# A sparse attention and feed-forward kernel: splitting its weights two tiles at a time

## The chip, the cores and the metric

The kernel runs on one core of one Trainium2 chip. The metric is the device time of one execution in microseconds (us), and lower is better. Shown with a kernel is the median of several executions; the profile is that of one further execution.

## The reference

Block-sparse attention over 4 batches, 8 heads, 768 positions and head size 64 is followed by a feed-forward layer over all 3072 tokens. Only the feed-forward part matters for the change:

```python
def _moe_ref(x, w_in, w_out):
    h = x @ w_in                                              # 3072x512 @ 512x2048
    sp = np.maximum(h, 0.0) + np.log1p(np.exp(-np.abs(h)))
    g = h * erf(sp)
    return (g @ w_out).astype(np.float32)                     # 3072x2048 @ 2048x512
```

The weights `w_in` and `w_out` are random float64 arrays. The attention output, with a batch's heads side by side, is `x`.

## The kernel before

**Precision.** TensorE multiplies f16 operands. So that little is lost, every f32 weight is scaled by a power of two and split into two f16 numbers: a high half, which is the rounded scaled weight, and a low half, which is what the rounding left. Three products (high by high, high by low, low by high) then stand for one.

**The weights.** Each weight is 16 tiles of 128 x 512. `weights()` (L512) is a generator that handles them in 17 steps, two neighbouring tiles (a pair) per step: steps 0 to 7 read `w_in`, steps 8 to 15 read `w_out`. A step decodes the float64 words to f32 on VectorE (`decode`, L418) and sums their squares on ScalarE (`square`, L437). From the sums come powers of two as scales: two for `w_in` (`scale_half`, L484, for 8 tiles each) and eight for `w_out`, one for each pair (`scale_pair`, L475, through a small TensorE matmul with ones, then `scale_part`, L469). `scale_part` runs three operations on a 128 x 1 column: exponent, scale and inverse scale. `ratios` (L488), after the last step, turns the inverse scales into the factors that `ff_gate` (L756) needs, and into `unscale` for the output.

**The split.** `halves` (L443) gives three views of tile i: the f32 tile, its high half and its low half. `high` (L451) is one ScalarE activation per tile, which copies with the scale from a 128 x 1 column and writes f16. For `w_out` the low half is one VectorE operation per tile (`low`, L455): weight times scale minus high half. For `w_in` the low half is made on TensorE: `rest` (L500) multiplies the f32 tile by a diagonal matrix of scales into PSUM, `rest_low` (L504) subtracts the high half by a matmul with minus the unit matrix, and `rest_out` (L507) copies the result out on ScalarE. The PSUM tag that `rest` and `scale_pair` use has two buffers.

**Places.** The halves are written over the buffer that holds the f32 weights. Slot n of a weight's buffer is 512 f32 wide. For `w_in` the f32 tile i lies in slot i + 1 and its halves go to slot i; for `w_out` the f32 tile lies in slot i + 2 (`APART`, L374). So the high half of `w_in` tile i + 1 overwrites a part of f32 tile i, and may be written only once `rest(i)` has read that.

**Order.** `weights()` is advanced three steps after each of the first six attention units (L917 to L940) and then run to its end (L944). Up to there, and through the first three rounds of the loop behind, a planner that simulates the engines chooses the order of TensorE, ScalarE and VectorE instructions; parts under `tc.high_priority()` go ahead. GpSimd and SyncE keep the order of the program. From round 3 of the main loop on (`held`, L960) all engines keep it.

**Main loop (L958).** Each round does `ff_first` (L710) for one group (24 matmuls into one of three PSUM tiles `h`), `ff_logs` (L734, five ScalarE activations, the first of which reads `h`), attention products of an older unit (`values`, L640), scores of a new one (`scores`, L608), `ff_second` (L765, 24 matmuls) for the group three rounds back, and `ff_gate` for the group two rounds back, whose first operation `y<-y,h` is the last reader of `h`. `gathers` (L807) brings the next blocks of V by DMAs that GpSimd and SyncE issue; a buffer for them is free when `values` has read it.

Of the kernel before, what the change touches and what calls it, by code (L numbers as in the profile page):

```python
# [10 lines left out]
I32 = mybir.dt.int32  # L11
BF16 = mybir.dt.bfloat16
AF = mybir.ActivationFunctionType
ALU = mybir.AluOpType
# [17 lines left out]
def sparse_attention_moe(ctx: ExitStack, tc: tile.TileContext, qT, kT, v, sampled, w_in, w_out, out):  # L32
# [7 lines left out]
    class InOrder:  # L40
# [15 lines left out]
    pe, act, dve, pool, sp = (  # L56
        InOrder(e, queued if e in (nc.sync, nc.gpsimd) else held) for e in (nc.tensor, nc.scalar, nc.vector, nc.gpsimd, nc.sync)
    )
# [54 lines left out]
    for n in range(P // BLOCK):  # L113
        part = slice(n * BLOCK, (n + 1) * BLOCK)
# [80 lines left out]
    def pow2_bound(bound, tag, by_sum):  # L195

        top = st.tile([P, 1], F32, tag="top", name=f"top_{tag}")
        dve.reduce_max(top, bound, AX.X)  # L200
        if by_sum:
            allm = ps_h.tile([P, W], F32, tag="h", name=f"allm_{tag}")
            if tag[0] == "v":
                pe.matmul(allm[0:1, 1 : 1 + P], top, eye, start=True, stop=True)
                top = st.tile([P, 1], F32, tag="top", name=f"most_{tag}")[0:1]
                dve.reduce_max(top, allm[0:1, 1 : 1 + P], AX.X)
            allm = allm[:, :1]
            pe.matmul(allm, ones[: top.shape[0]], top, start=True, stop=True)
        else:
            allm = st.tile([P, 1], F32, tag="allm", name=f"allm_{tag}")  # L210
            pool.partition_all_reduce(allm, top, P, bass.bass_isa.ReduceOp.max)
        return allm
# [161 lines left out]
    APART = {"i": 1, "o": 2}  # L374

    def weight_tile(name, n):
        return cp.tile([P, n + APART[name[1]], 512], F32, tag=name, name=name)

    NG = DFF // 512
    wi = weight_tile("wi", NK * NG)  # L380
    wo = weight_tile("wo", NF)
    wi16 = wi.rearrange("p n c -> p (n c)").bitcast(F16).rearrange("p (n c) -> p n c", c=1024)
    wo16 = wo.rearrange("p n c -> p (n c)").bitcast(F16).rearrange("p (n c) -> p n c", c=1024)
# [34 lines left out]
    def decode(key, i):  # L418

        first = i + APART[key]  # L420
        t = wi if key == "i" else wo
        w32 = t[:, first : first + 2, :].rearrange("p n c -> p (n c)")
        parts = [raw for n in (i, i + 1) for raw in places.pop((key, n), [])]
        mag = mags[(i // 2) % 2]
        c = 0
        for raw in parts:
            w = raw.shape[1] // 2
            raw = raw.rearrange("p (n w) -> p n w", w=2)
            lo, hi = raw[:, :, 0], raw[:, :, 1]
            m = mag[:, c : c + w]  # L430
            dve.tensor_scalar(m, hi, 3, 0x3FFFFFFF, ALU.logical_shift_left, ALU.bitwise_and)
            dve.scalar_tensor_tensor(m, hi, -0x40000000, m, ALU.bitwise_and, ALU.bitwise_or)
            done = w32[:, c : c + w].bitcast(I32)
            dve.scalar_tensor_tensor(done, lo, 29, m, ALU.logical_shift_right, ALU.bitwise_or)
            c += w

    def square(key, i):  # L437
        first = i + APART[key]
        w32 = (wi if key == "i" else wo)[:, first : first + 2, :].rearrange("p n c -> p (n c)")
        sq = mo.tile([P, 512], F32, tag="s", name=f"sq_{key}{i}", bufs=3).bitcast(BF16)  # L440
        act.activation(sq, w32, AF.Square, accum_out=wsq[key][:, i // 2 : i // 2 + 1])

    def halves(key, i):  # L443
        t, t16 = (wi, wi16) if key == "i" else (wo, wo16)
        return t[:, i + APART[key], :], t16[:, i, :512], t16[:, i, 512:]

    def scale_of(key, i):
        n = i // (2 * NK) if key == "i" else i // 2
        return (si if key == "i" else so)[:, n : n + 1]

    def high(key, i):  # L451
        w32, hi16, _ = halves(key, i)
        act.activation(hi16, w32, AF.Copy, scale=scale_of(key, i))

    def low(key, i):  # L455
        w32, hi16, lo16 = halves(key, i)
        dve.scalar_tensor_tensor(lo16, w32, scale_of(key, i), hi16, ALU.mult, ALU.subtract)

    NP = NF // 2
    eo, so, io = (sums[:, 16 + n * (NP + 2) : 16 + (n + 1) * (NP + 2)] for n in range(3))  # L460
    si, ii = so[:, NP:], io[:, NP:]
    sos, so = so, so[:, :NP]
# [4 lines left out]
    unit23 = float(1 << 23)  # L467

    def scale_part(total, n):  # L469
        e, sc, inv = eo[:, n : n + 1].bitcast(I32), sos[:, n : n + 1].bitcast(I32), io[:, n : n + 1].bitcast(I32)  # L470
        dve.tensor_scalar(e, total.bitcast(I32), 24, None, ALU.logical_shift_right)
        dve.tensor_scalar(sc, e, -unit23, (127 + 13 + 63) * unit23, ALU.mult, ALU.add)
        dve.tensor_scalar(inv, e, unit23, (127 - 13 - 63) * unit23, ALU.mult, ALU.add)

    def scale_pair(i):  # L475
        n = i // 2
        total = ps_o.tile([P, DM], F32, tag="o", name=f"total_{i}")[:, :1]
        pe.matmul(total, ones, wsq["o"][:, n : n + 1], start=True, stop=True)
        scale_part(total, n)

    def bound_part(part):
        return pow2_bound(wsq["i"][:, part * NK : (part + 1) * NK], f"wi{part}", True)

    def scale_half(total, part):  # L484
        scale_part(total, NP + part)
        dve.tensor_scalar(diag, eye, si[:, part : part + 1], None, ALU.mult)

    def ratios():  # L488
        dve.tensor_reduce(least[:, 0:1], si, AX.X, ALU.min)
        dve.tensor_scalar(rest_i, ii, least[:, 0:1], 2.0**-H_SHIFT, ALU.mult, ALU.mult)  # L490
        dve.tensor_reduce(least[:, 1:2], so, AX.X, ALU.min)
        for part in range(2):
            c = slice(part * NP // 2, (part + 1) * NP // 2)
            dve.tensor_scalar(ratio[:, c], io[:, c], least[:, 1:2], rest_i[:, part : part + 1], ALU.mult, ALU.mult)
        dve.tensor_scalar(least.bitcast(I32), least.bitcast(I32), -1.0, 254 * unit23, ALU.mult, ALU.add)
        dve.tensor_tensor(unscale, least[:, 0:1], least[:, 1:2], ALU.mult)
# [3 lines left out]
    def rest(i):  # L500
        rests[i] = ps_o.tile([P, DM], F32, tag="o", name=f"rest_{i}")
        pe.matmul(rests[i], diag, halves("i", i)[0], start=True, stop=False)

    def rest_low(i):  # L504
        pe.matmul(rests[i], less16, halves("i", i)[1], start=False, stop=True)

    def rest_out(i):  # L507
        act.activation(halves("i", i)[2], rests.pop(i), AF.Copy)
# [3 lines left out]
    def weights():  # L512
        loads = {5: (("o", 0),), 6: (("o", 2),), 7: (("o", 4), ("o", 6)), 10: (("o", 8),), 11: (("o", 10),)}
        sum_i = None
        for n in range(17):
            key, i = "io"[n // 8 % 2], n % 8 * 2
            if n in (4, 9):
                with tc.high_priority():
                    scale_half(sum_i, n // 8)
            pair = None  # L520
            if 5 <= n < 9:
                pair = 2 * (n - 5)
            if 10 <= n < 14:
                pair = 2 * (n - 6)
            if pair is not None:
                for part in range(2):
                    rest(pair + part)
                    high("i", pair + part)
            if n < 16:
                decode(key, i)  # L530
            if pair is not None:
                for part in range(2):
                    rest_low(pair + part)
                    rest_out(pair + part)
            if n < 16:
                square(key, i)
            if n >= 9:
                i = 2 * (n - 9)
                scale_pair(i)
                high("o", i)  # L540
                high("o", i + 1)
                low("o", i)
                low("o", i + 1)
            for piece in loads.get(n, ()):
                load_w(*piece)
            if n in (3, 7):
                sum_i = bound_part(n // 4)
            yield
        ratios()

    softs = {}
# [330 lines left out]
    def later(n=1):  # L882
        for _ in range(n):
            next(wgen, None)

    wgen = weights()
    for pr in range(HP):
        load_k(0, pr)
# [69 lines left out]
    for m in range(len(groups) + FF_LAG):  # L958
        ch, i = divmod(m, NGR)
        held[0] = m >= FF_LAG  # L960
        steps = 0
        if ch < len(until):
            first = until[ch - 1] if ch else FIRST
# [5 lines left out]
        last = groups[m - GATE_LAG] if GATE_LAG <= m < len(groups) + GATE_LAG else None  # L969
# [76 lines left out]
```

## Time and profile before

| | |
|---|---|
| median of 3 runs | 812.88 us (805.91 to 815.5) |
| the profiled execution | 810.12 us |
| its span, first to last instruction | 808.3 us |
| TensorE busy | 726.3 us (90%) |
| ScalarE busy | 601.6 us (74%) |
| VectorE busy | 560.3 us (69%) |
| GpSimd busy | 198.3 us (25%) |
| mean granted TensorE clock | 0.949 |

PE is TensorE's matmuls, PEld its weight loads, ACT is ScalarE, DVE is VectorE, POOL is GpSimd, SP is SyncE. The profile names an operation by its output and inputs in the program's tile names (`wi<-wi,sums` is `high` of `w_in`, `wo<-wo,sums` on ACT is `high` and on DVE `low` of `w_out`, `rest<-wi,room` is `rest` and `rest_low`). Nearly all rows carry L48, the line of a helper that issues everything, so one goes by tile names. The profiled execution was 2.76 us below the median of the three runs.

### The profile page before, as it was taken

The numbers are of one execution on the slowest core, as the hardware profiler recorded it, in microseconds if no ns is written. First come the engines' busy times: TensorE is split into PE (matmuls) and PEld (weight loads), VectorE is DVE, ScalarE is ACT, GpSimd is POOL, SyncE is SP. The second block draws the span as 40 slices with busy tenths as digits, with TensorE's granted clock in tenths as the row PEclk, the third lists the DMA queues.
The fourth block names the chain that finished last, engine by engine and source line by source line (L and its number), as shares of the span: only waits on it lengthen the run. The fifth ranks groups of instructions, "written<-read, shape, count | busy, mean of one in ns | idle before, by whom it ended". The sixth has DMA issues, their size and how long they took to land.

```text
span 808.3 us, 26228 instructions
## 1 busy us (share of the span) xinstructions
PE 726.3 (90%) x11136; PEld 510.3 (63%) x11136; DVE 560.3 (69%) x1043; ACT 601.6 (74%) x1035; POOL 198.3 (25%) x397
## 2 busy tenths in 40 slices
PE   1457787789978999999989999999999999999997
PEld 1435555556745776666767767667777776666663
DVE  7795898657756776766668768666767776564543
ACT  3656799567856788777867977877878878777674
POOL 3248410212333432400133423210333310000000
PEclk9558998979999999999999999999999999999999
DMA  9999654997499997953498997844598647312100
GB/s 315 398 258 294 202 116 76 145 241 166 119 218 182 171 274 185 203 132 81 92 206 182 215 212 185 190 97 98 130 191 180 149 113 181 73 28 48 9 27 26
DMA packets 188053, 129.45 MB, mean 160 GB/s; under 512 B 137760, under 2 KB 160928, under 8 KB 186912
## 3 DMA queue, kind: packets, MB, share of 16 engines
q1 hardware_dynamic: 173440, 83.98, 49.4%
q10 hardware_dynamic: 8608, 25.96, 10.7%
q0 software_dynamic: 5888, 17.84, 9.1%
q8 instruction: 87, 1.43, 0.7%
q14 instruction: 30, 0.25, 0.1%
HBM read 82.81 MB, written 12.95 MB: 118 GB/s over the span
## 4 chain that ended last, share of the span: by engine, by line
PE 74%; DMA 8%; issue 8%; DVE 5%; POOL 3%; ACT 1%; SPq 1%; POOLq 0%; ACTq 0%; DVEq 0%
PE h L48 29%; PE o L48 29%; PE s_m L48 8%; PE po_None L48 4%; PE s_f L48 3%; DMA qt<-in_qT_dram 2%; DMA xT<-x 2%; POOL kg L48 2%; DMA vbuf<-vtab,idx 1%; DVE room L48 1%; PE po L48 1%; DMA pT_f<-p_f 1%; DMA vbuf<-in_v_dram 1%; POOL vbuf L48 1%; DMA vtab<-vn 1%
## 5 line engine op out<-in xcount | busy, mean ns | idle before, releaser
L48 PE MATMUL h<-xT,wi 128*128 128x256 f16 x2304 | 276.8, 278 | 17.4 <-issue 8.4
L48 PEld LDWEIGHTS <-wi 128*128 128x128 f16 x2304 | 229.4, 100 | 69.2 <-issue 15.1
L48 PE MATMUL o<-wo,g 128*128 128x512 f16 x1152 | 266.5, 381 | 0.3 <-DVE g L48 0.2
L48 ACT ACTIVATE x<-x 128x512 f32<-128x512 f32 x288 | 181.5, 631 | 8.9
L48 PEld LDWEIGHTS <-g 128*128 128x128 f16 x1152 | 109.9, 98 | 122.3 <-issue 3.1
L48 POOL DMA_INDIRECT vbuf<-vtab,idx x88 | 91.2, 1037 | 333.2 <-PE po_None L48 263.9
L48 DVE SCALAR_TENSOR_TENSOR y<-y,x 128x512 f32<-128x512 f32 x96 | 68.4, 712 | 91.7 <-ACT x L48 91.5
L48 PE MATMUL s_m<-kx,qm 128*64 128x64 f32 (+1 forms) x1408 | 98.3, 251 | 31.8 <-DVE qm L48 14.5
L48 ACT ACTIVATE x<-h,isg 128x512 f32<-128x512 f32 x96 | 65.5, 682 | 59.0 <-PE h L48 58.6
L48 POOL COPY kg<-kx 128x128 f32 x264 | 88.7, 382 | 80.1 <-PE s_m L48 52.7
L48 PEld LDWEIGHTS s_m<-kx,qm 128*64 128x64 f32 x1408 | 73.4, 148 | 33.3 <-ACT sq_i L48 14.4
L48 ACT ACTIVATE pf_m<-s_m,less_m 128x256 f32<-128x256 f32 x176 | 69.0, 475 | 24.8 <-DVE less_m L48 22.4
L48 ACT ACTIVATE y<-y 128x512 f32<-128x512 f32 x96 | 59.7, 622 | 31.5 <-DVE y L48 25.8
L48 DVE TENSOR_REDUCE less_m<-s_m 128x4 f32<-128x1024 f32 x44 | 53.8, 1222 | 29.9 <-PE s_m L48 28.7
L48 DVE SCALAR_TENSOR_TENSOR g<-y,sums,g 128x512 f16<-128x512 f32 x96 | 72.1, 752 | 3.4
L48 PE MATMUL s_m<-kg,qm 128*64 128x96 f32 x704 | 68.5, 262 | 2.6 <-POOL kg L48 1.6
L48 DVE SCALAR_TENSOR_TENSOR y<-y,h 128x512 f32<-128x512 f32 x96 | 65.4, 681 | 0.5
L48 ACT ACTIVATE y<-x 128x512 f32<-128x512 f32 x96 | 60.5, 630 | 2.9
L48 PEld LDWEIGHTS s_m<-kg,qm 128*64 128x64 f32 x704 | 47.4, 149 | 8.0 <-issue 5.9
L48 DVE TENSOR_SCALAR g<-y,sums 128x512 f16<-128x512 f32 x96 | 47.0, 489 | 3.4
L48 PEld LDWEIGHTS <-pT_m 128*32 128x32 f16 x4224 | 38.5, 95 | 16.5 <-issue 13.0
L48 ACT ACTIVATE p_m<-pf_m 128x1024 f16<-128x1024 f32 x38 | 40.3, 1061 | 11.5 <-DMA pT_m<-p_m 5.8
(106 smaller groups left out, 618.4 us busy)
## 6 DMA issues: line engine op xcount, KB each, us to landing
vbuf<-vtab SPq DMA_DIRECT2D x80, 195.0 KB, 4.6
vraw<-in_v_dram ACTq DMA_DIRECT2D x9, 768.0 KB
vtab<-vn SPq DMA_DIRECT2D x16, 390.0 KB, 8.3
vbuf<-vtab SPq DMA_DIRECT2D x12, 520.0 KB, 4.0
wo<-in_w_out_dram ACTq DMA_DIRECT2D x6, 1024.0 KB
qt<-in_qT_dram SPq DMA_DIRECT2D x20, 256.0 KB, 5.3
kr<-in_kT_dram ACTq DMA_DIRECT2D x12, 384.0 KB, 5.4
vbuf<-vtab SPq DMA_DIRECT2D x32, 130.0 KB, 5.2
```

The lines of the kernel that those rows point to most:

```text
L48: done = call(*args, **kwargs)
```

## The change

One view, `both`, spans two neighbouring tiles. `high` is called once per pair, for both weights, and `low` once per pair for `w_out`. For a `w_in` pair, both `rest` calls now stand ahead of the one `high`. `scale_part` no longer forms the inverse scale: `invert` does it, for `w_in` once per half as before, and for the eight scales of `w_out` once, in `ratios`.

```diff
+    def both(key, i):
+        t, t16 = (wi, wi16) if key == "i" else (wo, wo16)
+        first = i + APART[key]
+        return t[:, first : first + 2, :], t16[:, i : i + 2, :512], t16[:, i : i + 2, 512:]
+
     def high(key, i):
-        w32, hi16, _ = halves(key, i)
+        w32, hi16, _ = both(key, i)
         act.activation(hi16, w32, AF.Copy, scale=scale_of(key, i))
 
     def low(key, i):
-        w32, hi16, lo16 = halves(key, i)
+        w32, hi16, lo16 = both(key, i)
         dve.scalar_tensor_tensor(lo16, w32, scale_of(key, i), hi16, ALU.mult, ALU.subtract)
...
     def scale_part(total, n):
-        e, sc, inv = eo[:, n : n + 1].bitcast(I32), sos[:, n : n + 1].bitcast(I32), io[:, n : n + 1].bitcast(I32)
+        e, sc = eo[:, n : n + 1].bitcast(I32), sos[:, n : n + 1].bitcast(I32)
         dve.tensor_scalar(e, total.bitcast(I32), 24, None, ALU.logical_shift_right)
         dve.tensor_scalar(sc, e, -unit23, (127 + 13 + 63) * unit23, ALU.mult, ALU.add)
-        dve.tensor_scalar(inv, e, unit23, (127 - 13 - 63) * unit23, ALU.mult, ALU.add)
...
+    def invert(first, last):
+        e, inv = eo[:, first:last].bitcast(I32), io[:, first:last].bitcast(I32)
+        dve.tensor_scalar(inv, e, unit23, (127 - 13 - 63) * unit23, ALU.mult, ALU.add)
+
     def scale_half(total, part):
         scale_part(total, NP + part)
+        invert(NP + part, NP + part + 1)
         dve.tensor_scalar(diag, eye, si[:, part : part + 1], None, ALU.mult)
 
     def ratios():
+        invert(0, NP)
         dve.tensor_reduce(least[:, 0:1], si, AX.X, ALU.min)
...
             if pair is not None:
                 for part in range(2):
                     rest(pair + part)
-                    high("i", pair + part)
+                high("i", pair)
...
                 scale_pair(i)
                 high("o", i)
-                high("o", i + 1)
                 low("o", i)
-                low("o", i + 1)
```

## Rows read from the trace of the kernel before

**Rows 1.** Busy time by stretch: PE, PEld, DVE, ACT, POOL, PEclk, DMA share, GB/s.

```profile
100.00:120.00 20.00, 16.09 (x210) 10.78 (x211) 18.49 (x44) 19.15 (x38) 4.92 (x10) 0.91 0.51 118
...
600.00:700.00 100.00, 100.00 (x1722) 71.77 (x1722) 71.30 (x131) 81.03 (x139) 21.23 (x38) 1.00 0.67 151
```

**Rows 2.** Chain that ended last, 113 to 260 us: start, length, what.

```profile
134.96 3.09 DMA vbuf<-vtab,idx
...
189.03 2.62 PE h L48 x24
```

**Rows 3.** Waits, 40 to 140 us: total us, times, longest.

```profile
POOL vbuf L48 <- PE po_None L48: 41.8, 5, 21.3
...
ACT wi L48 <- PE rest L48: 3.7, 5, 1.2
```

**Rows 4.** PE in order of time: start, length, what, idle before it.

```profile
113.27 3.83 PE L48 MATMUL h<-xT,wi 128*128 128x256 f16 x21 [1.20 <-DVE xT L48]
...
128.80 4.92 PE L48 MATMUL h<-xT,wi 128*128 128x256 f16 x24 [4.52 <-DVE y L48]
133.65 0.96 PE L48 MATMUL po_None<-vbuf,pT_m 128*32 128x65 f16 x96
```

**Rows 5.** ACT in order of time, around the first group's activations.

```profile
107.60 0.40 ACT L48 ACTIVATE xT<-turned 128x256 f16<-128x256 f32 x1
...
118.32 0.69 ACT L48 ACTIVATE x<-h,isg 128x512 f32<-128x512 f32 x1 [0.71 <-PE h L48]
...
119.91 1.33 ACT L48 ACTIVATE wo<-wo,sums 128x512 f16<-128x512 f32 x2
...
122.74 0.63 ACT L48 ACTIVATE x<-x 128x512 f32<-128x512 f32 x1
123.26 1.33 ACT L48 ACTIVATE wo<-wo,sums 128x512 f16<-128x512 f32 x2
...
125.52 1.33 ACT L48 ACTIVATE wo<-wo,sums 128x512 f16<-128x512 f32 x2
...
127.27 0.62 ACT L48 ACTIVATE y<-y 128x512 f32<-128x512 f32 x1
```

**Rows 6.** DVE in order of time, ahead of the first group.

```profile
102.44 0.18 DVE L48 TENSOR_SCALAR sums<-sums 128x1 int32<-128x1 int32 x2
102.55 0.15 DVE L48 TENSOR_SCALAR sums<-total 128x1 int32<-128x1 int32 x1
...
107.42 0.74 DVE L48 SCALAR_TENSOR_TENSOR wo<-wo,sums 128x512 f16<-128x512 f32 x1
108.08 1.02 DVE L48 SCALAR_TENSOR_TENSOR wo<-raw,room 128x512 int32<-128x512 int32 x2
...
112.81 0.42 DVE L48 SCALAR_TENSOR_TENSOR xT<-turned,xT 128x256 f16<-128x256 f32 x1
```

**Rows 7.** Instructions that write `wi` and `wo`: ns min/median/max, first and last start.

```profile
L48 ACT ACTIVATE wi<-wi,sums x16: 713/724/799, 55.1 to 113.6; 128x512 f16<-128x512 f32 x16
...
L48 ACT ACTIVATE wo<-wo,sums x16: 704/720/772, 91.7 to 129.5; 128x512 f16<-128x512 f32 x16
L48 DVE SCALAR_TENSOR_TENSOR wo<-wo,sums x16: 743/746/752, 94.7 to 131.1; 128x512 f16<-128x512 f32 x16
```

**Rows 8.** Costliest groups (page): busy us, mean ns of one, idle before.

```profile
L48 ACT ACTIVATE p_m<-pf_m 128x1024 f16<-128x1024 f32 x38 | 40.3, 1061 | 11.5 <-DMA pT_m<-p_m 5.8
```

**Rows 9.** Groups by shape, 0 to 200 us: busy us, mean ns.

```profile
L48 PE MATMUL rest<-wi,room 128*128 128x512 f32 x32 | 19.7, 714 | 2.9 <-ACT wi L48 2.5 <-DVE room L48 0.4
...
L48 DVE SCALAR_TENSOR_TENSOR pT_m<-turned,pT_m 128x512 f16<-128x512 f32 x12 | 8.1, 682 | 3.8 <-ACT pT_m L48 3.8
...
L48 DVE SCALAR_TENSOR_TENSOR p_m<-pf_m,p_m 128x1024 f16<-128x1024 f32 x5 | 6.1, 1218 | 0.0
```

**Rows 10.** Busy time by short stretch; columns as in Rows 1.

```profile
124.00:128.80 4.80, 0.28 (x5) 0.20 (x3) 4.79 (x15) 4.80 (x9) 0.00 (x0) 0.75 0.08 16
128.80:133.70 4.90, 4.90 (x32) 3.32 (x36) 3.62 (x7) 4.23 (x8) 0.00 (x0) 0.55 0.00 0
```

## Prediction

> **What bounds the kernel now.** I read the busy times by stretch first. From about 300 us on TensorE has no gap: 100.00 us busy of 100 between 600 and 700 us [rows 1]. The change touches nothing there, so it can only bring the start of that part forward or push it back. All splitting of weights lies between 55 and 132 us [rows 7]. There, between 100 and 120 us, ScalarE is busy 19.15 of 20 us and VectorE 18.49, while TensorE has gaps [rows 1].
>
> The chain that ended last tells which of this work counts. Read backwards, it is TensorE back to back down to 189 us (24 matmuls `h` in 2.62 us), with attention transfers before, down to a gather of V at 134.96 us [rows 2]. In front of that gather stands GpSimd, idle for 21.3 us; the waits name what ended it: a buffer of V that the matmuls `po` had to read first [rows 3]. Those matmuls are in TensorE's order of time at 133.65 us, behind a group `h` that began at 128.80, after 4.52 us in which TensorE waited for `y` of VectorE [rows 4]: with three PSUM tiles, the fourth group waits until the first one's last reader `y<-y,h` is done. That reader needs the first group's five activations and their exponential. ScalarE's order of time shows these from 118.32 to 127.27 + 0.62 = 127.89 us, with no idle time inside, and three pairs of `high` of `w_out` among them (119.91, 123.26, 125.52) [rows 5]. At 118.32 ScalarE had waited 0.71 us for the group `h` [rows 5], which began at 113.27, when VectorE's `xT` came [rows 4]; `xT` (112.81) stood in a full VectorE queue [rows 6].
>
> So the path here is: VectorE's queue to 112.81, TensorE's first group to 118.2, ScalarE's queue to 127.89, then `y`, `h`, `po`, the gather, and so on. An operation saved counts where it stands in one of these two queues.
>
> **The price of an edit.** *High halves.* Two in a row take 1.33 us where one takes 0.72 [rows 5, 7], so the second adds 0.61, and in a full queue a pair costs 1.22. The trace has no 128x1024 copy with a scale from a column. It has one with a constant scale that writes f16 in a strided pattern as well: `p_m`, 1.06 us [rows 8]. The column costs some 0.09 (0.72 with it, 0.63 for an equally wide activation without, [rows 5, 7]), and neighbours overlap by 0.72 - 0.61 = 0.11. So the wide one takes 1.06 + 0.09 - 0.11 = 1.04 us of the queue, and a pair saves 0.18. Bounds: without the column's price it would be 0.95 and save 0.27; at the price of two narrow ones it saves nothing. A loss is excluded by `p_m`: same size, same output type. I take 0.18, nearest to that row. Sixteen pairs save 2.9 us of ScalarE's time in all.
>
> *Low halves.* One takes 0.746 [rows 7], and the next operation starts 0.66 after it (107.42 to 108.08) [rows 6], so a pair costs 1.32. The 128x1024 form without a column takes 1.218, the 128x512 form without one 0.682 [rows 9]; with the column (0.746 - 0.682 = 0.06) and the overlap (0.746 - 0.66 = 0.09) the wide one takes 1.19. It saves 0.13 per pair (bounds 0 and 0.19, without the column), 1.0 us over eight.
>
> *Inverse scales.* Two column operations take 0.11 us of the queue (102.44 to 102.55) [rows 6], so one is about 0.06. Seven fewer give 0.4 us. The one that is left stands at the head of `ratios`, alone up to 0.15 us [rows 6] ahead of the factors for `g`. What TensorE waits for at 128.80 is `y` and not `g` [rows 4], so this has cover; without the cover it costs 0.15.
>
> **What of it lies on the path.** In VectorE's queue ahead of `xT`, between 102.44 and 112.81, stand one pair of low halves (107.42 and its neighbour) and at most two inverse scales: 0.13 + 2 x 0.06 = 0.25 us. In ScalarE's queue between 118.32 and 127.89: three pairs, 3 x 0.18 = 0.54 us. TensorE's own work is unchanged. Together 0.8 us; by the bounds 0 to 0.19 + 0.12 + 3 x 0.27 = 1.1. The other savings lie before 113 us in places where ScalarE waits for TensorE anyway (3.7 us in five waits of `wi` for `rest`, [rows 3]) or behind 127.89, or shorten queues whose end is set elsewhere. All that follows is started by the order of the program, so 0.8 us should arrive at the end. No DMA is added or moved; transfers of weights that reuse a buffer can only start a little earlier.
>
> The profiled execution was 810.12 us; 810.12 - 0.8 = 809.3. It lay 2.76 us below the median, so against the median the forecast is 812.88 - 0.8, about 812.1 us. A measurement of this kernel can tell about 1% (8 us) from no change; this is a tenth of that.
>
> **The added wait.** The wide `high` of a `w_in` pair writes over f32 tile i, so it must wait for `rest(i)`; before, only the second of the two narrow ones did. ScalarE takes its instructions in order, and what stands behind is exponentials, squares and copies for attention. In the waits this shows already: those 3.7 us. Before the change the first narrow copy could fill that time; now both halves wait. I expect the planner, which knows the wait, to put other work ahead, as the gapless queue after 118 us shows that there is enough.
>
> The Trainium skill ("TensorE: Matmul & The Clock Gate", section on the 16 sub-arrays) says that ScalarE and VectorE are strict first-in first-out queues. By that rule everything behind a waiting wide copy is late by the whole wait, which is the rival next but one; the 3.7 us agree that such waits happen, though only 0.74 us each.
>
> **Rivals.**
> *More comes off than the sum, through the clock and the order.* The group at 128.80 took 4.92 us, against 2.62 for the same 24 matmuls later [rows 2, 4], as the granted clock averaged 0.55 there, near the lower of the two levels, after a stretch with 0.28 us of matmuls in 4.80 [rows 10]. If that gap shrinks and the clock holds, 4.92 - 2.62 = 2.3 us go as well. And `xT` waits: its ScalarE part ended at 107.60 + 0.40, its VectorE part came at 112.81 [rows 5, 6]. A new order by the planner may take up to 4.8 us of that. All of it would give 812.9 - 0.8 - 2.3 - 4.8 = 805.0. Against it: 0.8 us off a gap of 4.52 leaves most of the gap, and nothing in the edit moves `xT` ahead.
> The Trainium skill (same page, "The HAM clock gate") says that an idle array is throttled and that sustained activity releases it; the low clock behind the gap agrees, and by that rule only a much shorter gap gives the 2.3 us.
>
> *The wide copy holds the queue: slower.* Each of the eight `w_in` pairs can add the wait for both passes of `rest` (2 x 0.714 = 1.43 us, [rows 9]) and the longer copy ahead of `rest_low` (1.06 + 0.09 - 0.72 = 0.43): 1.86 us. It decides against the kernel as soon as more than 0.8 us of the eight waits, one half of one wait, is uncovered on the path. Four pairs uncovered: 4 x 1.86 - 0.8 = 6.6 us more, 819.5; all eight: 14.1 more, 827. For it: ScalarE has hardly any idle time to give between 100 and 120 [rows 1]. Against: only the first pairs of `w_in` are needed early, and TensorE's gaps leave room to run `rest` ahead.
>
> *The edit does not do what it says:* a wide operation costs as much as two narrow ones, saving 0. Then 812.9. `p_m` at 1.06 against 1.22 speaks against it.
>
> **How the numbers follow.** Forecast 0.60, more through clock and order 0.16, held queue 0.18, nothing saved 0.06. Faster by over 1% (below 804.8) comes from the first rival's far end with other changes of order, 0.10, and 0.03 of the forecast's spread: 0.13. Slower by over 1% (above 821.0) is the held queue with five pairs or more, 0.10, and 0.02: 0.12. Within 1%: 0.75. The bounds of the sum move the time by 1 us only. The shown runs of before lie 10 us apart, and the two rivals reach to 805 and 820, so the range is 802 to 821.
>
> **What would show it.** In the profile after: 16 wide ScalarE copies of about 1.15 us and 8 wide VectorE operations of about 1.28 instead of 32 and 16; 8 column operations with `total` as now but 7 fewer on `sums`; ScalarE's busy time down by some 4 us (durations overlap, so more than the queue's 2.9) and VectorE's by 2; the first group's exponential 0.5 to 1 us earlier after its first activation; then GpSimd's long wait ends about 0.8 us sooner and TensorE's part after 300 us is unchanged. Wrong would be: long waits of `wi` for `rest` in ScalarE's order, the first group `h` more than 2 us from 113.27, or a group at 128.80 at the full clock.

## The result: a little slower

Over 20 executions each, the changed kernel takes 814.89 us (median) against 809.93: a ratio of 1.0068, with a 95% interval of 1.0044 to 1.0091. Three more comparisons of it gave 1.0024 (0.999 to 1.0058), 1.002 (0.9987 to 1.0054) and 1.0042 (1.0006 to 1.0078). So the loss is between 0.2% and 0.7%, some 1.5 to 5.5 us, and two of the four intervals take in no change. The forecast was 0.8 us faster. Comparisons leave out disturbed executions, so a ratio and the quotient of two medians need not agree.

The profiled execution after took 807.74 us (span 805.9), the lowest of the 20. Its end therefore says little about the loss; its start says much.

First the prices. Instructions that write `wi` and `wo` after, in ns min/median/max with first and last start:

```profile
L48 ACT ACTIVATE wi<-wi,sums x8: 1147/1150/1199, 60.0 to 128.1; 128x1024 f16<-128x1024 f32 x8
...
L48 ACT ACTIVATE wo<-wo,sums x8: 1137/1156/1194, 105.6 to 144.4; 128x1024 f16<-128x1024 f32 x8
L48 DVE SCALAR_TENSOR_TENSOR wo<-wo,sums x8: 1273/1280/1285, 108.7 to 146.2; 128x1024 f16<-128x1024 f32 x8
```

The wide forms cost what the forecast said, 1.15 and 1.28 us. The busy times of the page fell as well, ScalarE's from 601.6 to 597.1 and VectorE's from 560.3 to 557.5. But compare the last starts with [rows 7]: the last high half of `w_out` came at 129.5 and comes at 144.4, the last one of `w_in` at 113.6 and at 128.1. Less work ends later.

TensorE after, in order of time (start, length, what, idle before it), which answers to [rows 4]:

```profile
103.12 2.47 PE L48 MATMUL h<-xT,wi 128*128 128x256 f16 x21
...
116.37 1.88 PE L48 MATMUL rest<-wi,room 128*128 128x512 f32 x4
121.70 0.91 PE L48 MATMUL rest<-wi,room 128*128 128x512 f16 x2 [3.45 <-ACT wi L48]
124.17 0.58 PE L48 MATMUL total<-sums,room 128*128 128x1 f32 x2 [1.56 <-ACT wi L48]
124.66 3.78 PE L48 MATMUL rest<-wi,room 128*128 128x512 f32 x4
129.17 2.36 PE L48 MATMUL h<-xT,wi 128*128 128x256 f16 x20 [0.73 <-DVE y L48]
131.36 0.59 PE L48 MATMUL rest<-wi,room 128*128 128x512 f16 x2
...
132.64 0.38 PE L48 MATMUL total<-sums,room 128*128 128x1 f32 x2
...
133.44 0.38 PE L48 MATMUL total<-sums,room 128*128 128x1 f32 x2
...
134.97 0.38 PE L48 MATMUL total<-sums,room 128*128 128x1 f32 x2
...
138.71 2.84 PE L48 MATMUL o<-wo,g 128*128 128x512 f16 x12
141.39 2.78 PE L48 MATMUL h<-xT,wi 128*128 128x256 f16 x24
```

This is another order. The first group `h` starts 10 us earlier than in [rows 4] (the prediction had named a distance of more than 2 us as a sign of being wrong), yet the fourth starts where it did (129.17 against 128.80), as it needs a PSUM tile that the first must give back. What moved behind is the splitting of `w_in`: TensorE waits 3.45 us at `rest_low` for the wide copy, and the last four `rest` passes run at 124.66. With them moved the small `total` matmuls of `w_out`; those of the last four pairs stand behind the fourth group `h`. In the kernel before all of this is done earlier (TensorE before, in order of time):

```profile
118.23 0.38 PE L48 MATMUL rest<-wi,room 128*128 128x512 f16 x1
...
124.00 0.28 PE L48 MATMUL total<-sums,room 128*128 128x1 f32 x2
...
136.47 2.76 PE L48 MATMUL o<-wo,g 128*128 128x512 f16 x12
139.07 2.78 PE L48 MATMUL h<-xT,wi 128*128 128x256 f16 x24
```

ScalarE after, in order of time, shows why they could not come sooner:

```profile
120.47 1.19 ACT L48 ACTIVATE wi<-wi,sums 128x1024 f16<-128x1024 f32 x1
...
128.13 1.20 ACT L48 ACTIVATE wi<-wi,sums 128x1024 f16<-128x1024 f32 x1
...
131.78 0.60 ACT L48 ACTIVATE wi<-rest 128x512 f16<-128x512 f32 x1
...
132.79 0.59 ACT L48 ACTIVATE wi<-rest 128x512 f16<-128x512 f32 x1
```

`rest` and `total` share two PSUM buffers, so a `total` can be written only when a copy has emptied one. The two copies that empty them end at 132.38 and 133.38, and the next totals start at 132.64 and 133.44. VectorE after, in order of time, has the consequence: `ratios` and behind it the first `g`.

```profile
137.14 0.47 DVE L48 TENSOR_SCALAR sums<-sums 128x4 f32<-128x4 f32 x2
137.52 0.87 DVE L48 TENSOR_SCALAR g<-y,sums 128x512 f16<-128x512 f32 x2
```

The same two in VectorE's order before:

```profile
126.95 0.47 DVE L48 TENSOR_SCALAR sums<-sums 128x4 f32<-128x4 f32 x2
...
128.78 0.48 DVE L48 TENSOR_SCALAR g<-y,sums 128x512 f16<-128x512 f32 x1
```

The first `g` comes at 137.52 instead of 128.78. The first `o`, which needs it, starts at 138.71 instead of 136.47. In this profile attention scores fill TensorE up to then; in the three repeats below it stands still for `g` for 0.54 to 0.78 us. The fifth group `h` stands behind that `o` (141.39 against 139.07). The waits after answer to [rows 3] (total us, times, longest):

```profile
ACT wi L48 <- PE rest L48: 6.1, 7, 2.8
...
PE rest L48 <- ACT wi L48: 4.8, 2, 3.5
```

`wi` waited 3.7 us for `rest` before and waits 6.1 after. The late part is nearly as it was, full of TensorE work (columns as in [rows 1]):

```profile
600.00:700.00 100.00, 99.27 (x1594) 70.58 (x1591) 70.11 (x128) 78.75 (x136) 18.92 (x36) 1.00 0.65 142
```

### The profile page after: what moved, and what is told of

Same layout as the page of the kernel before. It is cut to its first block, busy times and chain, and to the rows that moved or that the text cites. A ratio compares the mean times of both kernels' runs of the same rounds, so it can differ in the third digit from the quotient of the medians.

```text
span 805.9 us, 26202 instructions
## 1 busy us (share of the span) xinstructions
PE 726.3 (90%) x11136; PEld 509.0 (63%) x11136; DVE 557.5 (69%) x1028; ACT 597.1 (74%) x1019; POOL 203.4 (25%) x397
## 4 chain that ended last, share of the span: by engine, by line
PE 73%; DVE 10%; DMA 7%; issue 5%; ACT 4%; SPq 1%; another core or an unknown queue 0%; ACTq 0%; DVEq 0%
PE h L48 28%; PE o L48 27%; PE s_m L48 9%; PE po_None L48 4%; PE s_f L48 3%; DMA qt<-in_qT_dram 2%; DMA vbuf<-vtab 2%; DMA wo<-in_w_out_dram 2%; DVE y L48 2%; PE po L48 1%; DVE g L48 1%; DVE less_m L48 1%; DVE vn L48 1%; PE rest L48 1%; DVE room L48 1%
## 5 line engine op out<-in xcount | busy, mean ns | idle before, releaser
L48 PE MATMUL h<-xT,wi 128*128 128x256 f16 x2304 | 267.7, 273 | 5.9 <-DVE y L48 5.8
L48 PEld LDWEIGHTS <-wi 128*128 128x128 f16 x2304 | 225.1, 98 | 55.1 <-issue 7.7
L48 PEld LDWEIGHTS <-g 128*128 128x128 f16 x1152 | 110.1, 99 | 124.9 <-issue 6.6
L48 POOL DMA_INDIRECT vbuf<-vtab,idx x88 | 95.5, 1085 | 330.3 <-PE po_None L48 264.0
L48 PE MATMUL s_m<-kx,qm 128*64 128x64 f32 (+1 forms) x1408 | 100.3, 249 | 32.9 <-DVE qm L48 14.5
L48 DVE SCALAR_TENSOR_TENSOR g<-y,sums,g 128x512 f16<-128x512 f32 x96 | 74.1, 772 | 3.4
L48 PE MATMUL po_None<-vbuf,pT_m 128*32 128x65 f16 (+1 forms) x4224 | 46.3, 197 | 7.5 <-issue 2.8
```

Source lines behind the costliest of these rows:

```text
L48: done = call(*args, **kwargs)
```

## The experiments

Theory A: the wide `w_in` copy must wait for `rest` of the pair's first tile; with that wait the planner finds another order, in which the last `rest` and `total` matmuls, and with them `ratios`, the first `g` and the first `o`, are late. Rivals: the loss lies in the late part (B), or the wide operations of `w_out` hold up the queues (C).

All marks below are start times in us from the profiles: the last high copy of `w_in`, the second pass of the last `total`, the first `g` and `o`; h5, h8 and h10 are the fifth, eighth and tenth group `h`. Above the line of dots stand the kernels of the main argument, below it those of the controls.

| kernel | last w_in copy | last total | first g | first o | h5 | h8 | h10 | ratio (95%) |
|---|---|---|---|---|---|---|---|---|
| before | 113.6 | 124.0 | 128.8 | 136.5 | 139.1 | 169.9 | 188.9 | |
| before, again | 115.5 | 125.7 | 130.4 | 138.1 | 140.7 | 165.4 | 181.9 | 1.0016 (0.9988 to 1.0043) |
| changed | 128.1 | 135.1 | 137.5 | 138.7 | 141.4 | 166.0 | 182.3 | 1.0068 (1.0044 to 1.0091) |
| changed, again | 129.2 | 138.1 | 140.5 | 141.1 | 144.3 | 169.0 | 186.9 | 1.0024 (0.999 to 1.0058) |
| changed, third | 129.0 | 137.9 | 140.3 | 140.9 | 144.2 | 169.0 | 186.6 | 1.002 (0.9987 to 1.0054) |
| changed, fourth | 129.2 | 136.2 | 138.6 | 139.1 | 142.4 | 167.2 | 185.4 | 1.0042 (1.0006 to 1.0078) |
| w_in only | 130.5 | 138.6 | 142.8 | 143.3 | 149.4 | 173.5 | 188.3 | 1.0056 (1.0022 to 1.009) |
| w_in only, 2 | 129.2 | 136.5 | 140.4 | 140.9 | 146.9 | 170.9 | 184.5 | 1.0104 (1.0068 to 1.0139) |
| narrow, with wait | 130.6 | 136.6 | 139.0 | 139.5 | 145.5 | 170.8 | 189.2 | 0.9999 (0.996 to 1.0038) |
| narrow, with wait, 2 | 128.1 | 134.1 | 136.5 | 137.0 | 143.0 | 168.5 | 187.0 | 1.0126 (1.0072 to 1.0181) |
| w_out and inverse | 113.0 | 123.2 | 128.1 | 135.4 | 138.0 | 162.6 | 179.1 | 1.0012 (0.9982 to 1.0043) |
| w_out and inverse, 2 | 114.4 | 124.5 | 129.5 | 136.7 | 139.3 | 163.2 | 177.6 | 0.9983 (0.9949 to 1.0018) |
| no overlap | 110.2 | 121.1 | 128.1 | 135.0 | 137.6 | 162.4 | 183.7 | 0.9995 (0.9961 to 1.0029) |
| no overlap, 2 | 110.1 | 120.6 | 127.5 | 135.8 | 138.4 | 162.2 | 179.7 | 1.0014 (0.9975 to 1.0053) |
| ... | | | | | | | | |
| before, no overlap (control) | 108.9 | 119.0 | 130.0 | 137.2 | 139.8 | 165.1 | 186.1 | 1.0042 (1.0014 to 1.0071) |
| changed, one total | 124.7 | 96.8 | 130.2 | 137.1 | 139.7 | 164.2 | 186.2 | 1.0039 (0.9998 to 1.008) |
| changed, one total, 2 | 125.6 | 97.6 | 131.1 | 138.0 | 140.6 | 164.8 | 186.7 | 1.0084 (1.0051 to 1.0117) |
| before, one total | 111.3 | 84.2 | 130.1 | 138.2 | 140.8 | 164.7 | 178.2 | 0.9945 (0.9905 to 0.9986) |
| high on VectorE | 115.9 | 128.0 | 135.4 | 136.0 | 139.3 | 164.7 | 181.1 | 0.9966 (0.9935 to 0.9997) |
| high on VectorE, 2 | 115.7 | 124.9 | 133.9 | 134.7 | 137.7 | 163.0 | 183.6 | 0.9982 (0.9943 to 1.0021) |

**The changed kernel again** (no edit), three times.

> The changed kernel once more, for a profile nearer to its median. Theory A (the wide high half of a w_in pair must wait for rest of the first tile; the planner's order then puts the last rests and the total matmuls behind the fourth group h, so ratios and the first g come some 9 us later): ratio 1.005 to 1.009; ratios near 137 us instead of 127, the fifth to seventh groups h 2 to 4 us later than in the kernel before (139.07, 147.21, 155.34). Rival B (the loss is in the late part of the kernel, by transfers or clock): those three groups are level with before, and the gap grows after 300 us.

> The changed kernel a third time, beside the ninth on the same chip: ratio 1.002 to 1.008, ratios between 137 and 141 us, fifth group h between 141 and 145.

> The changed kernel a fourth time, beside the seventeenth experiment: ratio 1.002 to 1.008, first g between 137 and 141 us.

The marks are late in all of them, so B falls as far as the start goes. The first of these ratios (1.0024) lies below what was expected, the second at its lower end, the third inside.

**Only w_in by pairs.** The edit is shown against the kernel before; `high2` is the wide copy of the change.

```diff
                 for part in range(2):
                     rest(pair + part)
-                    high("i", pair + part)
+                high2("i", pair)
```

> Only the high halves of w_in are formed by pairs; w_out and the inverse scales as before. Theory A: the whole loss is here, ratio 1.005 to 1.010, ratios near 137 us. Rival C (wide operations in the queues of w_out hold up the first groups' activations): no loss here, ratio 0.998 to 1.002.

> Only w_in by pairs, again. Theory A (the wait, the order, the late first o): ratio 1.003 to 1.009, and the slowest of these four; fifth group h behind 142 us. If the loss seen before was chance of the transfers: 0.998 to 1.002.

Slower by 0.56% and 1.04%: the loss is here. `ratios` comes even later than expected (141.8 and 139.3 us against 137). TensorE of the first of the two, in order of time:

```profile
138.50 0.38 PE L48 MATMUL total<-sums,room 128*128 128x1 f32 x2
...
143.34 1.04 PE L48 MATMUL o<-wo,g 128*128 128x512 f16 x2 [3.42 <-DVE g L48]
145.13 4.45 PE L48 MATMUL o<-wo,g 128*128 128x512 f16 x10 [0.75 <-DVE g L48]
149.37 2.87 PE L48 MATMUL h<-xT,wi 128*128 128x256 f16 x22
```

Here TensorE stands still for 3.42 us before the first `o`, and then ten matmuls take 4.45 us. Busy time of this kernel between 140 and 150 us (columns as in [rows 1]):

```profile
140.00:145.00 5.00, 1.04 (x2) 0.13 (x2) 4.89 (x15) 3.43 (x6) 0.00 (x0) 0.81 0.27 86
145.00:150.00 5.00, 4.87 (x14) 1.95 (x15) 4.96 (x12) 2.87 (x8) 0.00 (x0) 0.50 0.00 0
```

After a stretch in which TensorE is busy for 1.04 of 5 us the granted clock is 0.50, the lower of the two levels. In the changed kernel's fourth profile, where TensorE waits 0.78 us at this place, the same ten take 2.33 us:

```profile
139.12 0.60 PE L48 MATMUL o<-wo,g 128*128 128x512 f16 x2 [0.78 <-DVE g L48]
140.25 2.33 PE L48 MATMUL o<-wo,g 128*128 128x512 f16 x10 [0.52 <-DVE g L48]
```

So the longer gap costs about 2 us more than its own length, an estimate from these two profiles. The Trainium skill ("TensorE: Matmul & The Clock Gate", Part 1) says that an idle array is throttled to half; the 0.50 behind this gap agrees.

**w_out by pairs and one inverse**, `w_in` one tile at a time. The edit is shown against the changed kernel; `high1` is the narrow copy. Both `rest` of a pair still stand ahead of both copies, but only the second copy must wait for the first `rest`, as in the kernel before.

```diff
-                high("i", pair)
+                for part in range(2):
+                    high1("i", pair + part)
```

> The high and low halves of w_out by pairs and the inverse scales in one operation; high halves of w_in one tile at a time as before. Theory A: no loss, a ratio of 0.996 to 1.000 (the forecast's 0.8 us is 0.1%), ratios near 127 us. Rival C: the loss is here, ratio 1.004 or more.

> w_out by pairs and one inverse, w_in as before, again. Theory A: ratio 0.996 to 1.001, fifth group h 0.5 to 1.5 us ahead of the kernel before. If the wide copies of w_out cost as well: 1.003 or more.

C falls: no loss, and no gain that can be told from none. Nor is it the place of the two `rest` in the program that makes the loss. VectorE and TensorE of the first one, in order of time:

```profile
128.12 0.49 DVE L48 TENSOR_SCALAR g<-y,sums 128x512 f16<-128x512 f32 x1
```

```profile
128.14 4.46 PE L48 MATMUL h<-xT,wi 128*128 128x256 f16 x24 [4.49 <-DVE y L48]
135.36 2.76 PE L48 MATMUL o<-wo,g 128*128 128x512 f16 x12
137.96 2.78 PE L48 MATMUL h<-xT,wi 128*128 128x256 f16 x24
```

The order is nearly that of before. In this profile the fourth group is 0.66 us and the fifth 1.11 us ahead of the kernel before [rows 4]; in the second one they are 0.69 and 0.24 us behind it, so the expected 0.5 to 1.5 us ahead did not come again. The two profiles of the kernel before differ by 1.67 us at this place themselves: a gain of the forecast's 0.8 us can be neither shown nor excluded here.

**The change without the overlap.** With the f32 tiles of `w_in` two slots behind their halves, the wide copy writes over nothing that the pair's `rest` reads. The edit is shown against the changed kernel.

```diff
-    APART = {"i": 1, "o": 2}
+    APART = {"i": 2, "o": 2}
...
-            raw = slots(wi, 1 + 2 * i, 4) if i < 8 else slots(wo, 2 * i - 16, 4)
+            raw = slots(wi, 2 + 2 * i, 4) if i < 8 else slots(wo, 2 * i - 16, 4)
```

> The changed kernel with the f32 tiles of w_in two slots behind their halves instead of one, as for w_out, so that a wide high half writes over nothing that the pair's rest still reads and need not wait for it. The computation is the same. Theory A: the loss goes, ratio 0.990 to 1.001, ratios ahead of the fourth group's end. If the wide operation itself (its length, or both rests standing ahead of it) were the cause: ratio 1.005 or more as in the changed kernel.

> The changed kernel without the overlap and so without the wait, again. Theory A: ratio 0.996 to 1.001, fifth group h before 140 us. If something else of the change is slow: 1.003 or more.

All operations are as wide as in the change, both `rest` stand ahead of the copy, and no loss can be told from none (0.9995 and 1.0014), where w_in only, measured beside these two, lost 0.56% and 1.04%. The totals are done early (VectorE and TensorE of the first of the two):

```profile
123.24 0.48 DVE L48 TENSOR_SCALAR sums<-sums 128x4 f32<-128x4 f32 x2
128.08 0.49 DVE L48 TENSOR_SCALAR g<-y,sums 128x512 f16<-128x512 f32 x1
```

```profile
120.60 0.90 PE L48 MATMUL total<-sums,room 128*128 128x1 f32 x4 [0.24 <-ACT wi L48]
128.10 4.19 PE L48 MATMUL h<-xT,wi 128*128 128x256 f16 x24 [6.60 <-DVE y L48]
135.04 2.76 PE L48 MATMUL o<-wo,g 128*128 128x512 f16 x12
```

Its control is the same edit made to the kernel before:

> The kernel before with the f32 tiles of w_in two slots behind their halves, nothing else: the control for the fourth experiment. If that one lost nothing because its wide copy has no wait, this one gains little: 0.995 to 1.002. If the distance alone speeds the start up and only hid a loss from the wide copies, this one is clearly faster, 0.994 or less.

It came out slower, 1.0042 (1.0014 to 1.0071), which neither reading had foreseen. So the distance alone gains nothing; its marks are early up to h5 and its h10 is late (186.1). Why it costs something with narrow copies was not followed.

**Narrow copies with the wait.** Nothing is made wider; an added dependency makes both copies wait for the first `rest` (the edit against the kernel before).

```diff
-                    high("i", pair + part)
...
+                for part in range(2):
+                    high("i", pair + part, read[pair])
```

> The kernel before, all operations as narrow as there, but both high halves of a w_in pair are made to wait for rest of the pair's first tile, as the wide one must. Theory A (the wait, by the order that it leads the planner to): the loss is here without any wide operation, ratio 1.004 to 1.012, ratios behind 135 us and the fifth group h 3 us or more behind 139.07. If the length of the wide operation were what counts: ratio 0.998 to 1.003, the order of TensorE as before.

> The fifth experiment's kernel again: all operations as narrow as before, but both high halves of a w_in pair wait for rest of the pair's first tile. Theory A (the wait, by the order that it leads to): ratio 1.003 to 1.010, first g behind 137 us. If the width of the copy is needed for the loss: ratio 0.998 to 1.002.

In the first comparison the median of all 12 executions was 816.43 us against 811.8, but the ratio 0.9999: undecided. The second gave 1.0126. Both profiles have the late order, though the first `g` of the second came at 136.5 and not behind 137 as expected (TensorE of the second):

```profile
133.96 0.38 PE L48 MATMUL total<-sums,room 128*128 128x1 f32 x2
137.00 1.03 PE L48 MATMUL o<-wo,g 128*128 128x512 f16 x2 [2.66 <-DVE g L48]
138.80 4.45 PE L48 MATMUL o<-wo,g 128*128 128x512 f16 x10 [0.76 <-DVE g L48]
143.04 2.90 PE L48 MATMUL h<-xT,wi 128*128 128x256 f16 x24
```

The wait alone is enough for the late order, and in one of the two comparisons for a loss. The place of the two `rest`, which this edit moves as well, does not do it: it is the same in w_out and inverse, where the order is early.

**One total for all pairs**, to take the totals out of the change (the edit against the changed kernel). The scale of the first pair serves all eight; the seven other matmuls and their column operations are left out.

```diff
     def scale_pair(i):
+        if i:
+            return
...
-        scale_part(total, n)
+        e, sc = eo[:, :NP].bitcast(I32), sos[:, :NP].bitcast(I32)
+        dve.tensor_scalar(e, total.bitcast(I32).to_broadcast([P, NP]), 24, None, ALU.logical_shift_right)
```

> The changed kernel, but the scale of the first w_out pair is used for all eight pairs: one total matmul instead of eight (the seven others and their column operations are left out). The wide copies and their waits stay. If the loss goes through the totals, ratios and the first g: ratios before 130 us, first o before 137.5, fifth group h before 140.5, ratio 0.994 to 1.001. If the late rests or the full ScalarE queue by themselves delay the fourth and fifth group: first o behind 138.5, ratio 1.003 or more.

> The changed kernel with one total for all w_out pairs, again (seven totals and their column operations are left out). Theory A: ratio 0.994 to 1.001, so that the first comparison of it (1.0039) was chance. If it is 1.003 or more again, lateness of the first o does not carry the loss, and what does stands behind the fifth group.

> Control for the ninth experiment: the kernel before with one total for all pairs. If the totals cost time only where they are late, there is little to gain here: ratio 0.996 to 1.002. If leaving them out saves as much here as in the changed kernel: 0.994 or less.

The marks did what theory A said, the time did not. The first `o` is at 137.1 and 138.0, h5 at 139.7 and 140.6; yet the ratios are 1.0039 (0.9998 to 1.008) and 1.0084 (1.0051 to 1.0117). By what was set down before the second run, then, the lateness of the first `o` does not carry the loss here, and what does stands behind the fifth group. The kernel before with one total is faster, 0.9945 (0.9905 to 0.9986), which lies between its two readings and decides neither. In both profiles of the change with one total the time goes between the eighth and the tenth group `h`, 22 us where the kernel before with one total has 13.5. TensorE of the first, in order of time:

```profile
164.22 2.78 PE L48 MATMUL h<-xT,wi 128*128 128x256 f16 x24
176.42 4.94 PE L48 MATMUL h<-xT,wi 128*128 128x256 f16 x24 [6.63 <-DVE y L48]
186.16 2.78 PE L48 MATMUL h<-xT,wi 128*128 128x256 f16 x24
```

ScalarE of the same profile, which feeds that `y`:

```profile
173.84 1.12 ACT L48 ACTIVATE vn<-vraw,s_v 128x384 f16<-128x384 f32 x2 [3.08 <-DMA vtab<-vn]
```

There the next batch's V is split part by part, and the part shown stands 3.08 us behind the write of the part before it to memory. Every kernel here passes this place: in all twenty profiles the ninth group `h` starts 2.5 to 2.6 us after that part. And the long stretch is not peculiar to one total: no overlap, which loses nothing, has 21.3 us from h8 to h10 in its first profile, with a write almost as long. The chain that ended last (start, length, what) in that profile:

```profile
161.83 9.20 DMA vtab<-vn
...
173.63 5.28 PE h L48 x24
```

and in the first one of one total:

```profile
164.25 9.56 DMA vtab<-vn
```

So it is not shown that the late `ratios` carry the loss, and this experiment speaks against it. What this kernel still has of the change is the wait itself: its last `w_in` copy starts at 124.7 and 125.6, between the 128 to 131 of the others with the wait and the 109 to 116 of those without.

**High halves on VectorE**, an attempt at a faster kernel: the kernel w_out and inverse with the last six pairs' high halves of `w_out` moved off ScalarE.

```diff
-                high("o", i)
+                (high_dve if n >= 11 else high)("o", i)
```

> The third experiment's kernel (w_out by pairs, one inverse, w_in one tile at a time), with the last six pairs' high halves of w_out formed on VectorE instead of ScalarE. If ScalarE's queue bounds the first groups, as the forecast had it, their first y comes 1.5 to 3 us earlier than in the third experiment and the ratio is 0.994 to 0.999; if not, 0.999 or more.

> The eighth experiment's kernel again, as the fastest so far: ratio 0.994 to 0.999 if its gain is real, 0.999 to 1.002 if it was chance (its first groups were no earlier than in the third experiment).

0.9966 (0.9935 to 0.9997) and 0.9982 (0.9943 to 1.0021): the fastest that keeps the whole computation, by perhaps 2 us. The step behind it is not borne out. Its fourth group `h`, which waits for the first `y`, came at 129.3 in the first profile and at 127.9 in the second, where w_out and inverse has 128.1 and 129.5. Its gain has no shown cause. Its first `g` is as late as 135.4 and 133.9 without a loss.

**The kernel before again.**

> The kernel before, unchanged, for a second profile and for what two equal kernels show: ratio 0.997 to 1.003. If the 14.6 us between the seventh and eighth group h in the first profile belong to the kernel, they are here again; if to that execution, the distance is 7 to 8 us as in the other profiles.

1.0016, and 7.71 us between the seventh and eighth group: the 14.6 us of the first profile belonged to that execution. That is also why h8 and h10 of the first row of the table are odd ones.

## Why the prediction was wrong

**The prices held.** 1.15 and 1.28 us per wide form were forecast and measured; ScalarE's busy time fell by 4.5 us (forecast 4) and VectorE's by 2.8 (forecast 2). Where the order stays, as in the kernel w_out and inverse, the ratios of 1.0012 and 0.9983 leave room for the forecast's 0.8 us but do not show it. From the first group `h` to the fourth, where 0.54 us was to be saved on ScalarE, its two profiles take 15.4 and 15.1 us and those of the kernel before 15.5 each.

**The step that failed is "The added wait".** It saw that the wide `w_in` copy must wait for `rest` of the first tile, and priced that at nothing, because the planner, "which knows the wait", would put other work ahead. It did, and the order that came of it is the one that loses: it put the first three groups `h` ahead, though the fourth still had to wait for a PSUM tile, and left `rest`, which holds the two buffers that `total` needs, for later. The last `w_in` copy came at 128.1 us instead of 113.6, the last `total` at 135.1 instead of 124.0. Groups `h` put ahead are not the loss by themselves: no overlap starts its first one at 99.7. The sum had taken the order of the kernel before as given, and the cover of `ratios` too: "What TensorE waits for at 128.80 is `y` and not `g`". That was true of the old order; in the new one `g` comes 8.7 us later.

**The path that the sum followed kept its time.** The gather behind the matmuls `po` was to start 0.8 us sooner; GpSimd issues it at 134.55 us instead of 134.96, 0.4 sooner. What came late stands behind it: the next gather that waits for `po` is issued at 145.42 instead of 143.09. The prediction also read too much into one row: TensorE is not without a gap "from about 300 us on", as it is busy for 94.77 of the 100 us between 400 and 500. No term of the sum hangs on this.

**The slower rival** had the right instruction and the wrong price. It let the wait hold ScalarE's queue, pair by pair. The waits of `wi` for `rest` grew by only 2.4 us; what came was a new order.

**The size.** Over the eight profiles with the wait (changed, w_in only, narrow with wait) h8 stands at 169.4 us on average and h10 at 186.3. Over the four with the change's wide `w_out` and no wait (w_out and inverse, no overlap) they stand at 162.6 and 180.0. The two profiles of the kernel before have 169.9 and 165.4, then 188.9 and 181.9. That lateness is of the size of the loss or above it, and it does not all arrive: the ratios of the three kernels lie between 0.9999 and 1.0126. Between h8 and h10 lies the write of V. On the chains that pass through it, it takes 7.1 us in the changed kernel and w_in only, 9.2 in no overlap and 9.1 to 9.6 with one total, and the profiles of one kernel differ by 1 us at most. So it depends on the order as well, and a later start can be made up for here, or an early one lost.

**What is shown and what is open.** In all ten comparisons of kernels with the wait (those with one total among them) but one undecided (0.9999) the ratio is above 1, in six of them with an interval clear of 1, and in one of these without any wide operation. Of the five other kernels that differ from the one before and do not have it, four are not slower, one of them with every operation wide; the exception is the control, narrow copies at the larger distance, at 1.0042. So the loss is shown to come with `w_in` by pairs, and to go when the copy need not wait. That the last `rest` and the last copy of `w_in` are late with it is in every profile. How this reaches the end is open: with one total the late `ratios`, first `g` and first `o` were gone and the loss was not. One rival was not tested: that any edit which moves the planner's order gains or loses about half a per cent by chance, as the control (1.0042) and the kernel before with one total (0.9945) did without a wait. That all four kernels with the wait came out on the slow side, three of them in every comparison, speaks against it and does not exclude it.

## What to carry to other kernels

Where a planner sets the order, an edit's price is more than its instructions: ask which new dependency it has, and read the order of the built program before its time is measured. Widening an operation that works in place over a staggered buffer widens its hazards too; one more slot of distance removed this one. And cover that comes from the old order ("`y` is later than `g`") is worth nothing if the order can change. A mark that comes late is not yet the cause of a loss: when the late `ratios` were taken away, the time did not come back.

## What was not expected of the hardware

Executions of one and the same kernel spread by 0.8% to 3.1% (801.81 to 818.02 us, 2%, for the kernel before in the first comparison), far more than most parts of this change are worth. Comparisons on different chips differ as well: the kernel before had medians of 811.54 and 811.8 us on two chips and 797.23 to 800.15 on two others. Whether chip or time of measurement makes that difference was not followed. A single profile of such a kernel, here the fastest execution of 20, must not be read by its end. A gap of 3.42 us in TensorE's work cost twice: the ten matmuls behind it took 4.45 us at a granted clock of 0.50, against 2.33 behind a gap of 0.78.
